# Score matmuls of a top-k attention: the second parts of q stored twice, so that the contraction is 128 rows

## The chip, the cores and the metric

One core of one Trainium2 chip runs the kernel. The metric is the device time of one execution in microseconds (us). Three executions of the kernel before took 955.11, 954.19 and 959.35 us; the median is 955.11 us.

## What is computed

Attention over q, k, v of 2 batches, 8 heads, 576 positions and 64 numbers per head, in which every row of scores keeps only its 32 largest; its output (1152 tokens of 512 numbers) goes through a mixture layer with one expert of eight per token, and then through a mixture of four experts that all tokens use.

```python
scores = scale * np.matmul(q, k.transpose(0, 1, 3, 2))
kth = np.partition(scores, -top_k, axis=-1)[..., -top_k:-top_k + 1]
scores = np.where(scores >= kth, scores, -1e9)
...
attn = attn / (np.sum(attn, axis=-1, keepdims=True) + 1e-09)
x = np.matmul(attn, v)
...
h = np.maximum(x[mask] @ w1[e], 0.0)
out[mask] = gate_w[mask, None] * (h @ w2[e])
...
out += p[:, e:e + 1] * (np.maximum(x @ w1[e], 0.0) @ w2[e])
```

## The kernel before, in words

The 1152 tokens are nine tiles of 128. Tile 4 (`MIX`) holds the end of batch 0 and the start of batch 1. The tiles form three groups: (0, 1), (2, 3, 4) and (5, 6, 7, 8). The attention of group 0 runs alone at the start. After that the mixture layers of group g run on TensorE while the attention of group g+1 is laid between them, so that TensorE's instruction stream alternates between first layers (`hps`, L1120), second layers (`y`, L1093) and pieces of attention. The last group's layers run alone at the end.

**Precision by parts.** An fp32 operand is written as two parts (a rounded one and the rest), and a product is a sum of products of parts. In the mixture layers these are `whi`, `wlo` of the weights (ScalarE rounds at L996, GpSimd or VectorE subtracts at L1004) and `hhi`, `hlo` of the hidden values (ScalarE L1134, VectorE L1137). A second layer needs `hlo` two f-tiles (blocks of 128 hidden values) after it was made from.

**Attention.** The unit of work is a tile and a pair of heads, 36 units in all. For each unit:

- `q_tr` (L313 to L319) transposes the pair's parts of q on TensorE into the bank `qtp`, and `q_ev` (L321 to L335) copies them on ScalarE into `qs`.
- `sc_mm` (twice, once per head) calls `scores_mm` (L265 to L277): for each half of the 576 keys two matmuls of 288 columns (in tile 4 four, for its two batches) accumulate in the bank `sps`. The first contracts 128 rows: the first part of q, which stands twice, against k's two parts (64 rows each, stacked). The second contracts 64 rows: the second part of q against the first part of k alone. `sc_ev` (L460) copies the sums on ScalarE to `s_sb`.
- VectorE finds the 32 largest of each row by four rounds of MAX8 and MATCH_REPLACE8 (L472, L481), ScalarE takes the exponential, VectorE masks it (`e`, L494), ScalarE and GpSimd make two half-precision parts (`pbuf`), a DMA transposes them (`pt`, L523), and TensorE multiplies by v (`pv`, L548).

The banks of `qtp` and `sps` come from one pool with a single buffer (`ps_s`), so a transpose waits until the scores before it are copied out, and the other way round. The pool of `qs` has 4 buffers, that of the rows of q (`qrow`) one.

Per tile, `q_hi` (ScalarE, L302) rounds q into the first copy, `q_lo` (L307) has GpSimd subtract and ScalarE write the first part's second copy (L311). For tile 0 this is done by pieces in `q_part` (L617).

**Order.** `at_step(n, fn)` puts each piece in a plan by half steps, and the plan is written out in that order; an attention step is emitted whenever the cost estimate of the mixture layers (`pace`) says one is due. Unit j starts at b0 = 8j. Its `q_tr` is at b0-16, `q_ev` at b0-15, `sc_mm` at b0-5 and b0-3, each `sc_ev` one step later; a tile's `q_hi` is at b0-21 and `q_lo` at b0-20 of its first unit. Each engine runs its instructions strictly in the order written.

```python
for n, r in ((i, slice(0, 128)), (2, slice(64 * i, 64 * i + 64))):
    nc.tensor.matmul(out=ps[:, f, 0:HALF], lhsT=qq[r, n, :],
                     rhs=kst[r, h, b * S + f * HALF:b * S + (f + 1) * HALF],
                     start=(j == 0), stop=(j == n_mm - 1))
```

Of the kernel before, what the change touches and what calls it, by code (L numbers as in the profile page):

```python
# [49 lines left out]
def kernel(  # L50
# [41 lines left out]
    def h_bank(shape, name):  # L92
        """A bank for a first layer's sums."""
        return ps_h.tile(shape, F32, tag="h", name=name)

    def side_bank(shape, name):
        """A bank for a side job's sums: of its own where there is one."""
        if not h_extra:
            return h_bank(shape, name)
        h_count[0] += 1  # L100
        return h_extra[h_count[0] % len(h_extra)].tile(shape, F32, tag="h", name=name)

    with tc.manual_schedule():
# [44 lines left out]
        def emit_const_math():  # L148
# [10 lines left out]
            # how many tokens each slot has room for: all, or its windows' rows; nothing beyond the slots  # L159
# [60 lines left out]
        def attention(at, start):  # L220
# [6 lines left out]
            qst_p = pool("qst", 4)  # L227
# [37 lines left out]
            def scores_mm(t, h, i, qs):  # L265
                ps = ps_s.tile([128, 2, 512], F32, tag="s", name="sps")
                bs = batches(t)
                for f in range(2):
                    n_mm = 2 * len(bs)
                    j = 0  # L270
                    for qq, b in zip(qs, bs):
                        for n, r in ((i, slice(0, 128)), (2, slice(64 * i, 64 * i + 64))):
                            nc.tensor.matmul(out=ps[:, f, 0:HALF], lhsT=qq[r, n, :],  # L273
                                             rhs=kst[r, h, b * S + f * HALF:b * S + (f + 1) * HALF],
                                             start=(j == 0), stop=(j == n_mm - 1))
                            j += 1
# [13 lines left out]
            # rows of q, k, v: load, split, transpose  # L290
# [6 lines left out]
            # q by pairs of heads: the first part of each twice, then the second parts; against k's two parts, which  # L297
            # an odd head has the other way round
            def q_first(t, n):
                return row["q", t][:, :, 0:4, :].rearrange("p c (i a) d -> p c i a d", a=2)[:, :, :, n, :]  # L300

            def q_hi(t):  # L302
                row["q", t] = row_p.tile([128, H // 2, 6, D], F32R, tag="qrow", name="qrow")
                nc.scalar.activation(out=q_first(t, 0), in_=raw["q", t].rearrange("p (c i) d -> p c i d", i=2),
                                     func=ACTF.Copy)

            def q_lo(t, eng):  # L307
                eng.tensor_tensor(out=row["q", t][:, :, 4:6, :],
                                  in0=raw.pop(("q", t)).rearrange("p (c i) d -> p c i d", i=2),
                                  in1=q_first(t, 0).bitcast(F32), op=ALU.subtract)  # L310
                nc.scalar.activation(out=q_first(t, 1), in_=q_first(t, 0).bitcast(F32), func=ACTF.Copy)  # L311
# [9 lines left out]
            def q_ev(j):  # L321
                t, hp = units[j]
                ps = st[j].pop("qps")
                if t != MIX:
                    qs = qst_p.tile([128, 3, 128], F32R, tag="qs", name="qs")
# [4 lines left out]
                for b in range(2):  # L330
                    qs = qst_p.tile([128, 3, 128], F32R, tag="qs", name=f"qs{b}")
# [87 lines left out]
            def v_scale(b, n):  # L419
                """The scale and its inverse, from the bound's exponent; the instructions apart."""  # L420
# [32 lines left out]
            # per pair of heads  # L453
# [102 lines left out]
            def row_factor(t, n):  # L556
                """The rows' factor, its three instructions apart."""
# [25 lines left out]
            # the first pair, by pieces: head 0's block of k, the two heads' last columns, head 1's block  # L583
            def first_ld():
# [19 lines left out]
                row["q", t] = row_p.tile([128, H // 2, 6, D], F32R, tag="qrow", name="qrow")  # L604
# [12 lines left out]
            def q_part(cs, part, eng=None):  # L617
                t = units[0][0]
                q0 = raw["q", t].rearrange("p (c i) d -> p c i d", i=2)[:, cs]
                if part == 1:  # L620
                    eng.tensor_tensor(out=row["q", t][:, cs, 4:6, :], in0=q0, in1=q_first(t, 0)[:, cs].bitcast(F32),
                                      op=ALU.subtract)
                else:
                    nc.scalar.activation(out=q_first(t, part // 2)[:, cs], in_=q0, func=ACTF.Copy)

            # the first pair's chain, and what it needs
            for n, fn, *args in (
                    (-40, first_ld), (-37, k_ld, 1, 0), (-34, emit_const_loads),
                    (-30, k_part, 0, 0), (-29, k_part, 0, 1), (-30, q_part, slice(0, 1), 0),
                    (-29, q_part, slice(0, 1), 1, nc.vector), (-29, q_part, slice(0, 1), 2),  # L630
                    (-28, k_part, 2, 0), (-27, k_part, 2, 1),
# [4 lines left out]
                    (-22, q_part, slice(1, H // 2), 1, nc.gpsimd),  # L636
# [5 lines left out]
            for j in range(NP):  # L642
# [73 lines left out]
        # what goes between VectorE's instructions that wait for one another, and whether side jobs go twice as often  # L716
# [3 lines left out]
        def gate(g, xhi, xlo, i0, i1):  # L720
            """Expert choice and gate of tiles i0..i1 of the group, and their counts."""
# [747 lines left out]
```

## Time and profile before

| | kernel before |
|---|---|
| time, median of 3 (lowest to highest) | 955.11 us (954.19 to 959.35) |
| profiled execution: span, first to last instruction | 952.8 us |
| TensorE matmul busy | 873.3 us, 92% |
| TensorE weight load busy | 707.2 us, 74% |
| VectorE busy | 662.1 us, 69% |
| ScalarE busy | 489.0 us, 51% |
| GpSimd busy | 535.7 us, 56% |
| DMA | 129.60 MB, mean 136 GB/s |
| mean granted TensorE clock | 0.955 of full |

The median is 2.3 us over the span of the profiled execution, whose own time beyond its span isn't given. In the profile PE is TensorE's matmuls, PEld its weight loads, DVE VectorE, ACT ScalarE, POOL GpSimd, SP the queue that issues most DMAs. L273 is line 273 of the kernel. Matmul ends are modelled: the distance between starts tells more than one matmul's length. A busy share is an average over the whole run; the stages below have different limits.

### The profile page before, as it was taken

To read this page: it belongs to the slowest core of one execution; us is meant where nothing else is said; L and a number is where in the kernel's file an instruction comes from. 1 tells how busy PE (TensorE), PEld (TensorE's weight loads), DVE (VectorE), ACT (ScalarE), POOL (GpSimd) and SP (SyncE) were. 2 spreads that over 40 slices of the span, in tenths; PEclk is the share of its full clock that TensorE was granted. 3 is DMA by queue.
4 is the path that set the end of the run, shared out by engine and by line. 5 is a ranking of instruction groups with operands and counts; after the bars stand their busy time and mean duration, and the time that the engine had idled before them with its cause. 6 is when DMAs were issued, how large, how long until landed. Compare 5 with 4: busy or idle time off the path is not lost.

```text
span 952.8 us, 15053 instructions
## 1 busy us (share of the span) xinstructions
PE 873.3 (92%) x5241; PEld 707.2 (74%) x5241; DVE 662.1 (69%) x1309; ACT 489.0 (51%) x1007; POOL 535.7 (56%) x469
## 2 busy tenths in 40 slices
PE   5776677999999998899999999997999999999996
PEld 3554465887877886788877888786889778888884
DVE  5998979998968999799979888974334341112222
ACT  5766654665766654567735665442356332422320
POOL 3553456886766976567857665573535533343330
PEclk9995578999999999799999999999999999999999
DMA  7354544766655663847756555453546622323201
GB/s 129 70 107 91 133 115 120 207 184 166 161 146 130 167 184 108 203 139 218 208 128 170 139 132 136 138 146 100 165 144 222 188 89 96 104 89 111 89 23 49
DMA packets 197627, 129.60 MB, mean 136 GB/s; under 512 B 129122, under 2 KB 172130, under 8 KB 197540
## 3 DMA queue, kind: packets, MB, share of 16 engines
q1 hardware_dynamic: 196500, 125.12, 48.7%
q0 software_dynamic: 1040, 3.41, 1.4%
q8 instruction: 43, 0.70, 0.3%
q14 instruction: 44, 0.36, 0.1%
HBM read 98.62 MB, written 6.30 MB: 110 GB/s over the span
## 4 chain that ended last, share of the span: by engine, by line
PE 77%; DVE 11%; DMA 3%; issue 2%; ACT 2%; SPq 2%; POOL 2%; POOLq 0%; ACTq 0%; DVEq 0%
PE hps L1120 31%; PE y L1093 30%; PE sps L273 8%; PE pv L548 4%; DVE m L472 3%; DVE w L481 3%; PE xtp L1022 1%; PE qtp L318 1%; DMA wraw<-in_moe_w_dram 1%; DMA xg<-x_scr,ixi 1%; PE ktp L370 1%; DVE e L494 1%; DMA pt<-pbuf 1%; POOL wlo L1004 1%; SPq L399 0%
## 5 line engine op out<-in xcount | busy, mean ns | idle before, releaser
L1004 POOL TENSOR_TENSOR wlo<-wraw,whi 128x512 fp32r<-128x512 f32 x278 | 368.9, 1346 | 282.2 <-ACT whi L996 236.1
L1137 DVE SCALAR_TENSOR_TENSOR hlo<-hps,hhi 128x256 fp32r<-128x256 f32 (+3 forms) x168 | 84.0, 500 | 210.0 <-ACT hhi L1134 209.7
L1134 ACT ACTIVATE hhi<-hps 128x256 fp32r<-128x256 f32 (+3 forms) x168 | 75.4, 449 | 268.5 <-PE hps L1120 260.5
L996 ACT ACTIVATE whi<-wraw 128x512 fp32r<-128x512 f32 x336 | 193.3, 624 | 23.0 <-DMA wraw<-in_moe_w_dram 22.8
L1093 PE MATMUL y<-whi,hhi 128*128 128x512 f32 x440 | 180.7, 411 | 0.0
L1120 PE MATMUL hps<-x,whi 128*128 128x256 f32 (+2 forms) x768 | 168.4, 342 | 6.4 <-DVE hlo L1137 5.1
L1093 PE MATMUL y<-wlo,hhi 128*128 128x512 f32 x440 | 173.5, 394 | 0.0
L1093 PE MATMUL y<-whi,hlo 128*128 128x512 f32 x440 | 173.1, 394 | 0.0
L472 DVE MAX8 m<-w 128x8 f32<-128x576 f32 x216 | 154.1, 743 | 0.0
L1120 PEld LDWEIGHTS hps<-x,whi 128*128 128x128 f32 x768 | 130.2, 191 | 21.2 <-DVE hlo L1137 5.5
L273 PE MATMUL sps<-kst,qs 128*128 128x288 f32 x320 | 120.7, 432 | 15.7 <-ACT qs L326 7.9
L518 POOL TENSOR_TENSOR pbuf<-e,pbuf 128x576 f16<-128x576 f32 (+1 forms) x80 | 107.2, 1340 | 47.6 <-ACT pbuf L509 45.0
L273 PEld LDWEIGHTS sps<-kst,qs 128*128 128x128 f32 x320 | 67.2, 210 | 66.6 <-issue 22.0
L481 DVE MATCH_REPLACE8 w<-m,w 128x576 f32<-128x576 f32 x144 | 105.9, 739 | 0.0
L1093 PEld LDWEIGHTS y<-whi,hlo 128*128 128x128 f32 x440 | 83.1, 189 | 18.5
L1093 PEld LDWEIGHTS y<-whi,hhi 128*128 128x128 f32 x440 | 83.8, 190 | 17.0
L1093 PEld LDWEIGHTS y<-wlo,hhi 128*128 128x128 f32 x440 | 83.7, 190 | 11.9
L1120 PE MATMUL hps<-x,wlo 128*128 128x256 f32 (+2 forms) x384 | 85.3, 341 | 0.0
L494 DVE SCALAR_TENSOR_TENSOR e<-s_sb,m,e 128x576 f32<-128x576 f32 x72 | 80.1, 1139 | 2.0 <-ACT e L489 2.0
L1120 PEld LDWEIGHTS hps<-x,wlo 128*128 128x128 f32 x384 | 65.8, 192 | 5.4
L548 PEld LDWEIGHTS <-pt 128*128 128x128 f16 (+3 forms) x1200 | 49.2, 106 | 27.1 <-issue 14.1
L548 PE MATMUL pv<-vst,pt 128*128 128x64 f16 (+3 forms) x1200 | 62.1, 204 | 6.1 <-DMA pt<-pbuf 4.8
(179 smaller groups left out, 1044.1 us busy)
## 6 DMA issues: line engine op xcount, KB each, us to landing
wraw<-in_moe_w_dram SPq DMA_DIRECT2D x168, 512.0 KB, 3.8
x_scr<-xrow SPq DMA_DIRECT2D x9, 256.0 KB, 2.0
out_dram<-acc SPq DMA_DIRECT2D x9, 256.0 KB, 2.2
kraw<-in_k_dram SPq DMA_DIRECT2D x16, 128.0 KB, 3.2
vraw<-in_v_dram SPq DMA_DIRECT2D x8, 256.0 KB, 3.4
qraw<-in_q_dram SPq DMA_DIRECT2D x7, 256.0 KB, 5.6
y_scr<-yr SPq DMA_DIRECT2D x6, 256.0 KB, 2.8
pt<-pbuf SPq DMA_TRANSPOSE x72, 4.1
```

What stands on the lines that cost most here:

```text
L273: nc.tensor.matmul(out=ps[:, f, 0:HALF], lhsT=qq[r, n, :], rhs=kst[r, h, b * S + f * HALF:b * S + (f + 1) * HALF], start=(j == 0), stop=(j ...
L472: nc.vector.max(out=z["m"][:, i, 8 * r:8 * r + 8], in_=z["s", i] if r == 0 else z["w"][i])
L481: nc.vector.match_replace(out=z["w"][i], in_to_replace=z["m"][:, i, 8 * r:8 * r + 8], in_values=z["s", i] if r == 0 else z["w"][i], imm_va ...
L494: nc.vector.scalar_tensor_tensor(out=z["e"][i], in0=z["s", i], scalar=z["m"][:, i, TOPK - 1:TOPK], in1=z["e"][i], op0=ALU.is_ge, op1=ALU.mult)
L518: nc.gpsimd.tensor_tensor(out=pb[r, 1, o:o + S], in0=z["e"][i][r], in1=pb[r, 0, o:o + S], op=ALU.subtract)
L548: nc.tensor.matmul(out=po[r, h, :], lhsT=l, rhs=rr, start=(n == 0), stop=(n == len(mms) - 1))
L996: nc.scalar.activation(out=hi, in_=src, func=ACTF.Copy)
L1004: eng.tensor_tensor(out=lo, in0=src, in1=hi.bitcast(F32), op=ALU.subtract)
L1093: nc.tensor.matmul(out=ys[i][0:rows, :], lhsT=l[:, cs], rhs=r[:, 0, :], start=(f == f0 and m == 0), stop=(f == f1 - 1 and m == 2))
L1120: nc.tensor.matmul(out=hp[:, 0:n], lhsT=l[:, c, :], rhs=r[:, c, x0:x0 + n], start=(m == 0), stop=(m == 3 * KD - 1))
L1134: nc.scalar.activation(out=hhi, in_=hp[:, 0:n], func=ACTF.Relu)
L1137: nc.vector.scalar_tensor_tensor(out=hlo, in0=hp[:, 0:n], scalar=0.0, in1=hhi.bitcast(F32), op0=ALU.max, op1=ALU.subtract)
```

## The change

The rows of q hold the second part twice as well (8 blocks of 64 per pair of heads where 6 stood). So there are four transposes per unit where three stood, `qs` is a third wider, and the second matmul of each pair is the same shape as the first: 128 rows, the second part of q against both parts of k. It so adds the product of the two second parts, which the kernel before left out. A new ScalarE copy, `q_two`, writes the second copy. `qs` has 3 buffers where it had 4. For tile 4 and the first unit of tile 5 `q_tr` moves from b0-16 to b0-9, and tile 5's `q_hi` and `q_lo` from b0-21 and b0-20 to b0-16 and b0-15. Comments and docstrings are emptied as well.

```diff
-            qst_p = pool("qst", 4)
+            qst_p = pool("qst", 3)
...
-                        for n, r in ((i, slice(0, 128)), (2, slice(64 * i, 64 * i + 64))):
-                            nc.tensor.matmul(out=ps[:, f, 0:HALF], lhsT=qq[r, n, :],
-                                             rhs=kst[r, h, b * S + f * HALF:b * S + (f + 1) * HALF],
+                        for n in (i, 2 + i):
+                            nc.tensor.matmul(out=ps[:, f, 0:HALF], lhsT=qq[:, n, :],
+                                             rhs=kst[:, h, b * S + f * HALF:b * S + (f + 1) * HALF],
...
-            def q_first(t, n):
-                return row["q", t][:, :, 0:4, :].rearrange("p c (i a) d -> p c i a d", a=2)[:, :, :, n, :]
+            def q_at(t, part, n):
+                return row["q", t].rearrange("p c (m i a) d -> p c m i a d", i=2, a=2)[:, :, part, :, n, :]
...
-                row["q", t] = row_p.tile([128, H // 2, 6, D], F32R, tag="qrow", name="qrow")
+                row["q", t] = row_p.tile([128, H // 2, 8, D], F32R, tag="qrow", name="qrow")
...
+            def q_two(t):
+                nc.scalar.activation(out=q_at(t, 1, 1), in_=q_at(t, 1, 0).bitcast(F32), func=ACTF.Copy)
...
-                ps = ps_s.tile([128, 3, 128], F32, tag="s", name="qtp")
+                ps = ps_s.tile([128, 4, 128], F32, tag="s", name="qtp")
...
-                for n in range(3):
+                for n in range(4):
...
-                    qs = qst_p.tile([128, 3, 128], F32R, tag="qs", name="qs")
+                    qs = qst_p.tile([128, 4, 128], F32R, tag="qs", name="qs")
...
+                elif part == 3:
+                    nc.scalar.activation(out=q_at(t, 1, 1)[:, cs], in_=q_at(t, 1, 0)[:, cs].bitcast(F32),
+                                         func=ACTF.Copy)
...
+                    (-28, q_part, slice(0, 1), 3),
...
-                    (-22, q_part, slice(1, H // 2), 1, nc.gpsimd),
+                    (-22, q_part, slice(1, H // 2), 1, nc.gpsimd), (-20, q_part, slice(1, H // 2), 3),
...
-                    at_step(b0 - 16 if j > 1 else -4, q_tr, j)
-                    at_step(b0 - 15 if j > 1 else -3, q_ev, j)
+                    late = t == MIX or (t == MIX + 1 and hp == 0)
+                    b2 = -4 if j == 1 else b0 - 9 if late else b0 - 16
+                    at_step(b2, q_tr, j)
+                    at_step(b2 + 1, q_ev, j)
...
-                    at_step(b0 - 21, q_hi, t)
-                    at_step(b0 - 20, q_lo, t, nc.gpsimd)
+                    b3 = b0 - 16 if t == MIX + 1 else b0 - 21
+                    at_step(b3, q_hi, t)
+                    at_step(b3 + 1, q_lo, t, nc.gpsimd)
+                    at_step(b3 + 3, q_two, t)
```

## Rows read from the trace of the kernel before

**Rows 1.** The page, part 4: the chain that ended last, shares by engine.

```profile
PE 77%; DVE 11%; DMA 3%; issue 2%; ACT 2%; SPq 2%; POOL 2%; POOLq 0%; ACTq 0%; DVEq 0%
```

**Rows 2.** Stages: length, busy PE, PEld, DVE, ACT, POOL (instructions), clock, DMA share, GB/s.

```profile
170.00:240.00 70.00, 68.59 (x494) 56.56 (x492) 62.88 (x119) 44.54 (x96) 52.97 (x43) 1.00 0.66 177
240.00:356.00 116.00, 115.22 (x884) 92.17 (x883) 101.56 (x203) 73.31 (x163) 89.83 (x72) 1.00 0.62 162
400.00:500.00 100.00, 97.75 (x655) 80.07 (x655) 91.30 (x164) 60.80 (x127) 67.36 (x55) 0.97 0.65 176
500.00:612.00 112.00, 110.96 (x692) 90.58 (x692) 99.47 (x190) 63.43 (x129) 72.26 (x62) 1.00 0.54 138
```

**Rows 3.** The chain in order of time, 312 to 340 us: start, length, instructions.

```profile
312.71 2.41 PE sps L273 x8
...
326.87 1.11 PE sps L273 x4
327.97 0.89 PE y L1093 x3
328.87 1.43 PE hps L1120 x12
330.30 0.69 PE y L1093 x3
...
339.15 0.48 PE qtp L318 x3
```

**Rows 4.** Timeline of TensorE's weight loads, 326 to 329 us: start, length, instructions.

```profile
326.93 0.83 PEld L273 LDWEIGHTS sps<-kst,qs 64*128 64x128 f32 x3 [0.26 <-issue]
...
328.48 0.65 PEld L1120 LDWEIGHTS hps<-x,whi 128*128 128x128 f32 x4
```

**Rows 5.** The score matmuls (L273) alone in the stages: length, PE, PEld, clock, DMA share, GB/s.

```profile
170.00:240.00 70.00, 11.54 (x36) 6.58 (x36) 1.00 0.66 177
240.00:356.00 116.00, 25.90 (x80) 14.79 (x80) 1.00 0.62 162
400.00:500.00 100.00, 14.54 (x44) 8.27 (x43) 0.97 0.65 176
500.00:612.00 112.00, 16.51 (x52) 9.62 (x52) 1.00 0.54 138
```

**Rows 6.** VectorE's waits, 170 to 240 us: waiter, releaser, us in total, times, longest.

```profile
DVE wlo L1004 <- ACT whi L996: 1.8, 1, 1.8
DVE x L1027 <- ACT x L1024: 1.7, 2, 1.4
```

**Rows 7.** VectorE's waits, 240 to 356 us.

```profile
DVE hlo L1137 <- ACT hhi L1134: 8.0, 8, 2.0
DVE wlo L1004 <- ACT whi L996: 2.7, 1, 2.7
DVE lg L740 <- PE lp L737: 1.9, 1, 1.9
```

**Rows 8.** VectorE's waits, 400 to 500 us.

```profile
DVE wlo L1004 <- ACT whi L996: 2.7, 2, 2.3
DVE xs L929 <- ACT xs L928: 2.3, 1, 2.3
DVE x L1027 <- ACT x L1024: 1.6, 2, 0.8
```

**Rows 9.** The chain at 23 and 154 us.

```profile
23.32 2.21 PE sps L273 x4
...
154.52 2.93 PE hps L1120 x12
```

**Rows 10.** VectorE's waits, 0 to 25 us.

```profile
DVE m L472 <- ACT s_sb L460: 4.6, 2, 2.3
```

**Rows 11.** Timelines of ScalarE and of GpSimd: tile 3's parts of q.

```profile
143.34 0.64 ACT L311 ACTIVATE qrow<-qrow 128x512 fp32r<-128x512 f32 x1
...
147.02 1.27 POOL L308 TENSOR_TENSOR qrow<-qraw,qrow 128x512 fp32r<-128x512 f32 x1
```

More of the change, by code (lines that the diff above doesn't have):

```diff
@@ L295, in ld @@
                 raw[kind, t] = load_rows(src, t, io_p, kind + "raw")
-            def q_first(t, n):
-                return row["q", t][:, :, 0:4, :].rearrange("p c (i a) d -> p c i a d", a=2)[:, :, :, n, :]
+            def q_at(t, part, n):
+                return row["q", t].rearrange("p c (m i a) d -> p c m i a d", i=2, a=2)[:, :, part, :, n, :]
             def q_hi(t):
-                row["q", t] = row_p.tile([128, H // 2, 6, D], F32R, tag="qrow", name="qrow")
-                nc.scalar.activation(out=q_first(t, 0), in_=raw["q", t].rearrange("p (c i) d -> p c i d", i=2),
+                row["q", t] = row_p.tile([128, H // 2, 8, D], F32R, tag="qrow", name="qrow")
+                nc.scalar.activation(out=q_at(t, 0, 0), in_=raw["q", t].rearrange("p (c i) d -> p c i d", i=2),
                                      func=ACTF.Copy)
             def q_lo(t, eng):
-                eng.tensor_tensor(out=row["q", t][:, :, 4:6, :],
+                eng.tensor_tensor(out=q_at(t, 1, 0),
                                   in0=raw.pop(("q", t)).rearrange("p (c i) d -> p c i d", i=2),
-                                  in1=q_first(t, 0).bitcast(F32), op=ALU.subtract)
-                nc.scalar.activation(out=q_first(t, 1), in_=q_first(t, 0).bitcast(F32), func=ACTF.Copy)
+                                  in1=q_at(t, 0, 0).bitcast(F32), op=ALU.subtract)
+                nc.scalar.activation(out=q_at(t, 0, 1), in_=q_at(t, 0, 0).bitcast(F32), func=ACTF.Copy)
+            def q_two(t):
+                nc.scalar.activation(out=q_at(t, 1, 1), in_=q_at(t, 1, 0).bitcast(F32), func=ACTF.Copy)
             def q_tr(j):
                 t, hp = units[j]
-                ps = ps_s.tile([128, 3, 128], F32, tag="s", name="qtp")
+                ps = ps_s.tile([128, 4, 128], F32, tag="s", name="qtp")
                 qf = row["q", t][:, hp].rearrange("p a d -> p (a d)").bitcast(F32)
-                for n in range(3):
+                for n in range(4):
                     nc.tensor.transpose(out=ps[:, n, :], in_=qf[:, n * 128:(n + 1) * 128], identity=ident)
@@ L330, in q_ev @@
                 for b in range(2):
-                    qs = qst_p.tile([128, 3, 128], F32R, tag="qs", name=f"qs{b}")
+                    qs = qst_p.tile([128, 4, 128], F32R, tag="qs", name=f"qs{b}")
                     z0, c0 = (64, 0) if b == 0 else (0, 64)
@@ L603, in first_ld @@
                 row["k", 0, 0] = k_p.tile([128, 5, 4, D], F32R, tag="krow", name="krow")
-                row["q", t] = row_p.tile([128, H // 2, 6, D], F32R, tag="qrow", name="qrow")
+                row["q", t] = row_p.tile([128, H // 2, 8, D], F32R, tag="qrow", name="qrow")
             def k_part(n, part):
@@ L620, in q_part @@
                 if part == 1:
-                    eng.tensor_tensor(out=row["q", t][:, cs, 4:6, :], in0=q0, in1=q_first(t, 0)[:, cs].bitcast(F32),
+                    eng.tensor_tensor(out=q_at(t, 1, 0)[:, cs], in0=q0, in1=q_at(t, 0, 0)[:, cs].bitcast(F32),
                                       op=ALU.subtract)
+                elif part == 3:
+                    nc.scalar.activation(out=q_at(t, 1, 1)[:, cs], in_=q_at(t, 1, 0)[:, cs].bitcast(F32),
+                                         func=ACTF.Copy)
                 else:
-                    nc.scalar.activation(out=q_first(t, part // 2)[:, cs], in_=q0, func=ACTF.Copy)
+                    nc.scalar.activation(out=q_at(t, 0, part // 2)[:, cs], in_=q0, func=ACTF.Copy)
             for n, fn, *args in (
```

## The prediction

> **What bounds the kernel now.** I read the chain that ended last, then the busy times by stage, then the waits in each stage. The chain lies on TensorE for 77% of the span and on VectorE for 11% [rows 1]. By stages TensorE is close to full from 170 to 240, 240 to 356, 400 to 500 and 500 to 612 us: it is idle for 1.4, 0.8, 2.3 and 1.0 us there. VectorE is behind it by little: it is idle for 7.1, 14.4, 8.7 and 12.5 us in the same stages [rows 2]. So two engines are nearly balanced while attention and mixture layers run together: whatever TensorE saves there counts only until VectorE has no idle time left. Before 154 us the top-k on VectorE sets the pace, between 356 and 400 us the routing does, and after 612 us no attention is left that the change could touch.
>
> **What a score matmul costs.** In the chain, twelve first-layer matmuls of 256 columns take 1.43 us, 0.119 us each, and three second-layer ones of 512 columns take 0.69 us, 0.23 us each [rows 3]. On the line through both, 288 columns of 128 rows take 0.119 + 32/256 x 0.111 = 0.133 us. The four matmuls of a score call take 1.11 us, and the three `y` behind them 0.89 where 0.69 is usual. A call so costs 1.31 us, more than twice what its columns need. The excess goes with the alternation of 128 and 64 rows: the weight load for a 64-row matmul sits idle for 0.26 us before it starts, while four loads of the first layer, all 128 rows, go in 0.65 us [rows 4].
>
> The Trainium skill, TensorEngine Tiling (Array Packing), Key Properties, says that a change of tiling mode, not of the tile alone, drains TensorE; it agrees with these rows.
>
> After the change every matmul on that path has 128 rows, so I take the 128-row price: 4 x 0.133 = 0.53 us a call, a saving of 0.78 us. Bounds: nothing if the wait belongs to the weights and not to the rows (a rival below), and the whole 0.78. I take the whole, since the first-layer rows are the nearest in shape and in parts. A call of tile 4 has eight matmuls: 2.41 us plus the same 0.20 behind it, less 8 x 0.133, saves 1.55 us [rows 3].
>
> **Parts of the sum, stage by stage.** The score matmuls number 36, 80, 44 and 52 in the four stages [rows 5]; tile 4's 64 fall into the second. That is 9 plain calls, 4 plain and 8 of tile 4, 11 and 13 plain. TensorE saves 7.0, 3.1 + 12.4 = 15.5, 8.6 and 10.1 us. Each unit (two calls) pays a fourth transpose. Three take 0.48 us in the chain [rows 3], so 0.16 us; over 4.5, 6, 5.5 and 6.5 units 0.7, 1.0, 0.9 and 1.0 us. Net on TensorE: 6.3, 14.5, 7.7 and 9.1 us, together 37.6 us.
>
> Now what VectorE lets through. Of its idle time I keep the waits whose releaser is not sped up. These are 1.8 us for rounded weights and 1.7 us for rounded rows in the first stage [rows 6], so 3.6 us of 7.1 can go. In the second they are 2.7 and 1.9 us [rows 7], so 9.8 us of 14.4 can go; 8.0 us of that waits for ScalarE's `hhi`, which waits for TensorE, so it is the kind of wait that a faster TensorE shortens. In the third they are 2.7, 2.3 and 1.6 us [rows 8], so 2.1 us of 8.7. In the fourth I keep none, and TensorE's 9.1 us is the smaller number. Taking the smaller of the two engines in each stage: 3.6 + 9.8 + 2.1 + 9.1 = 24.6 us.
>
> **The start.** There the clock is at its low level of 1.2 GHz by the durations: a score call takes 2.21 us, and twelve first-layer matmuls 2.93 us, 0.244 each [rows 9], so 288 columns about 0.275 and a call 1.1 us, a saving of 1.1 us. VectorE's first two MAX8 wait 4.6 us for the first two calls [rows 10]. Two savings come to 2.2 us, less one cold transpose and a wider copy in the first chain (by the rows for the warm ones some 0.4 us): 1.8 us. Later in this stage VectorE is what is waited for, and I count nothing: 23 calls get cheaper there behind the top-k.
>
> **ScalarE and GpSimd.** `q_two` is a copy of 128x512 for each tile, 0.64 us like the one that already stands there [rows 11]. A wider `q_ev` adds less than that per unit. ScalarE is idle for 43 of 116 us and 49 of 112 us in the fullest stages [rows 2], so I cost both at nothing; without that cover it would be at most 8 x 0.64 us, and some tenths per unit. But `q_two` also adds a wait: ScalarE can't go on until GpSimd has subtracted. Behind it in ScalarE's queue are `whi`, `hhi` and `s_sb`, and TensorE waits for those. For tile 3 GpSimd ends at 148.3 us, and ScalarE's copy before it starts at 143.3 us [rows 11]. `q_two` comes two steps after that copy; a unit of eight steps takes 70/4.5 = 15.6 us by rows 5, so it comes 3.9 us later, at 147.2 us. The wait is some 1.1 us for this tile, and VectorE is the bound there; I count nothing.
>
> **The moved steps.** For tile 4 and the first unit of tile 5 the transpose is four steps before the scores, some 8 us, instead of eleven; the copies in between are four of a few tenths, so they stay hidden. At tile 5 two transposes follow each other through the one bank, and TensorE must wait for ScalarE's copy between them. I price that once, 1 us, from the 0.64 us copy plus its place in the queue. The three buffers of `qs` hold as many bytes as the four before and, with tile 4's later steps, are free in time. `q_ev` waiting for a buffer is bounded by one score call, 1.3 us, at one place. Transfers, bytes and DMA issues are unchanged.
>
> **Sum.** 24.6 + 1.8 - 1.0 = 25.4 us off a profiled span of 952.8 us. The runs stand 2.3 us above the span; carried over, the median of 955.1 becomes 929.7, and I say 929 us.
>
> **Rivals.**
>
> *All of TensorE's saving arrives.* VectorE may run late without harm, because `hlo` is used two f-tiles later. Then 37.6 + 1.8 and about 2 us between 356 and 400 come off: 914 us. For it: VectorE's lateness has room inside a stage. Against: at the end of each stage the rows of the next layer need VectorE. Chance 0.10.
>
> *Less fits.* The same copies, subtractions and top-k come closer together, GpSimd is busy for 90 of 116 us already [rows 2], and weights come later. If only half of 25.4 us gets through: 942 us. Chance 0.13.
>
> *The load, not the rows.* The weight load of a matmul may have to wait until the matmul before it has left the same rows. Then 128-row matmuls pay a load (0.65/4 = 0.16 us at the least, [rows 4]) plus 0.133, about 0.30 us as now, nothing is saved, and 36 transposes of 0.16 us are added, of which the 22.5 in the four stages matter: 955 to 959 us. Against it, the first layers are 128 rows each and go at 0.119 us with their loads, less than one load and one matmul in series. The Trainium skill, TensorE: Matmul & The Clock Gate, Part 3: Packing small matmuls — row/col tiling, says that weight loads overlap with running matmuls only where the row groups differ; that speaks against the change and would give this time. The trace disagrees, with the 0.119 us of the first layers. Chance 0.03.
>
> *Slower.* `q_two` holds ScalarE. GpSimd's subtraction for tile 3 begins 3.7 us after ScalarE's neighbouring copy [rows 11]; if in a fuller schedule it begins some 5 us later still at each of seven tiles, ScalarE stands for 5 us each time, `hhi` and `whi` come late, and 35 us are lost against 25 won: 965 us. It decides where GpSimd ends more than about 4 us after that copy starts, and by more than two f-tiles' worth of slack. Against: the tile in the rows is over that by one us only. Chance 0.05.
>
> **How the numbers follow.** The forecast, 920 to 938 us around 929, has 0.69. The range of 913 to 945 us takes in the two neighbours on the fast side and leaves out the last two rivals and a tail on each side, together under 0.2. About 0.5% is what a measurement of this kernel can tell from no change. Faster by more: 0.69 + 0.10 + 0.13, less a little for a half that shrinks further: 0.90. Same: 0.04. Slower: 0.06.
>
> **What would show it right or wrong.** Right: score matmuls of one shape, 128 rows, x320; a call in the warm stages at about 0.53 us; no idle of 0.26 us before their loads; `y` behind them at 0.69 us for three; 144 transposes. VectorE's idle in the stage of tile 4 shrinks to about 5 us, its waits for `hhi` nearly go, and TensorE begins to wait for `hlo`. ScalarE's `q_two` waits for GpSimd by about a microsecond at most. The stages before 154 us and after 612 us keep their lengths but for the first microseconds. Wrong: calls that stay near 1.1 us (the load), long waits of ScalarE at `q_two`, a granted clock below 1.00 in the four stages, or a total at 914 us with VectorE still idle.

## The result, and the profile after

The changed kernel takes 924.9 us (median of 4 runs, 922.85 to 927.44) where the kernel before, on the same chip, takes 954.85 (4 runs, 954.19 to 959.35): a ratio of 0.9681, 95% interval 0.9653 to 0.971. The forecast was 929, with a range of 913 to 945.

The page of the changed kernel, parts 1 and 5: the span, the busy times, and the score matmuls as one group (busy us, mean ns, then idle before and its releaser).

```profile
span 921.1 us, 15133 instructions
...
PE 815.3 (89%) x5277; PEld 696.2 (76%) x5277; DVE 659.2 (72%) x1309; ACT 496.6 (54%) x1017; POOL 534.6 (58%) x469
...
L273 PE MATMUL sps<-kst,qs 128*128 128x288 f32 x320 | 64.8, 333 | 19.5 <-ACT s_sb L465 9.5
```

All 320 score matmuls now have one shape. TensorE's busy time fell from 873.3 to 815.3 us, 58.0 us, of which 31.7 reached the span (952.8 to 921.1). VectorE and GpSimd are busy as long as before, ScalarE 7.6 us longer. The spans are those of one execution each; by the medians the gain is 30 us. The question is where the other 26 us went.

TensorE's timeline after the change: a plain call at 515 us, and one of tile 4 at 258 us.

```profile
258.34 1.23 PE L273 MATMUL sps<-kst,qs 128*128 128x288 f32 x8
259.41 0.39 PE L1107 MATMUL y<-whi,hhi 128*128 128x512 f32 x1
...
515.10 0.69 PE L273 MATMUL sps<-kst,qs 128*128 128x288 f32 x4
515.62 0.85 PE L1134 MATMUL hps<-x,whi 128*128 128x384 f32 x4
```

The four weight loads of the plain call:

```profile
514.87 0.68 PEld L273 LDWEIGHTS sps<-kst,qs 128*128 128x128 f32 x4
```

Read the starts. The plain call takes 515.62 - 515.10 = 0.52 us, where 1.11 and 0.20 behind it stood [rows 3]; the call of tile 4 takes 259.41 - 258.34 = 1.07 us, where 2.41 and 0.20 stood. That is 0.13 us for each matmul of 128 rows and 288 columns. Their four loads go in 0.68 us without an idle stretch between them.

To see where the time came off, cut both traces where the same work happens: the transposes of a tile's rows of x (`xtp<-xrow`) and those of a group's sums (`xtp<-acc`). Stages of the kernel before: the start to tile 1's rows, tile 1's rows to group 0's sums, tile 2's rows to tile 4's, tile 4's rows to group 1's sums (in two pieces), tile 5's rows to tile 7's. Columns as in [rows 2].

```profile
0.00:126.88 126.88, 87.26 (x445) 58.39 (x445) 111.75 (x250) 79.31 (x163) 55.59 (x81) 0.79 0.52 107
126.88:234.10 107.22, 98.18 (x658) 81.46 (x659) 94.79 (x189) 64.29 (x139) 84.81 (x68) 0.94 0.62 167
239.98:355.45 115.47, 114.69 (x880) 91.65 (x878) 101.03 (x202) 73.33 (x163) 89.85 (x72) 1.00 0.62 162
355.45:400.00 44.55, 36.88 (x241) 30.78 (x239) 39.51 (x94) 22.29 (x50) 28.00 (x24) 0.91 0.56 142
400.00:492.64 92.64, 92.64 (x612) 76.20 (x611) 85.57 (x156) 57.72 (x121) 66.08 (x54) 0.97 0.70 190
500.68:590.69 90.01, 88.97 (x547) 72.63 (x545) 79.22 (x149) 51.53 (x104) 59.08 (x51) 1.00 0.56 144
```

The same stages of the changed kernel.

```profile
0.00:120.98 120.98, 67.42 (x457) 53.97 (x457) 110.37 (x250) 81.82 (x167) 56.83 (x81) 0.63 0.55 112
120.98:223.96 102.98, 91.05 (x661) 79.63 (x662) 94.27 (x189) 64.70 (x137) 83.20 (x68) 0.92 0.64 164
230.19:339.81 109.62, 102.69 (x886) 89.52 (x884) 101.32 (x201) 75.79 (x167) 89.39 (x72) 0.98 0.67 171
339.81:383.00 43.19, 36.63 (x253) 31.62 (x252) 40.16 (x97) 23.91 (x52) 28.89 (x25) 0.92 0.52 144
383.00:471.07 88.07, 82.24 (x609) 71.69 (x607) 84.59 (x154) 57.48 (x120) 64.30 (x54) 1.00 0.80 200
481.21:561.89 80.68, 80.68 (x551) 71.64 (x550) 76.72 (x145) 51.94 (x104) 57.71 (x49) 1.00 0.56 150
```

| from and to (before) | length before, after | came off |
|---|---|---|
| start to tile 1's rows, 0 to 126.88 | 126.88, 120.98 | 5.9 |
| to group 0's sums, 234.10 | 107.22, 102.98 | 4.2 |
| to tile 2's rows, 239.98 | 5.88, 6.23 | -0.4 |
| to tile 4's rows, 355.45 | 115.47, 109.62 | 5.9 |
| to group 1's sums, 492.64 | 137.19, 131.26 | 5.9 |
| to tile 5's rows, 500.68 | 8.04, 10.14 | -2.1 |
| to tile 7's rows, 590.69 | 90.01, 80.68 | 9.3 |
| to the end | 362.1, 359.2 | 2.9 |

TensorE's busy time tells where the rest went. In the stages from tile 1's rows to tile 7's it fell by 7.1, 12.0, 10.7 (both pieces) and 8.3 us, 38.1 in all, where 37.6 was forecast for four stages cut a little otherwise; 25.3 of that came off. At the start it fell by 19.8 us, and 5.9 came off.

In the last of the full stages TensorE is still busy throughout (80.68 of 80.68 us), and all of its saving arrives. In the stage of tile 4 it is now idle for 6.9 us where it was idle for 0.8, and of 12.0 us that it saved 5.9 arrive. The waits of TensorE in that stage after the change (waiter, releaser, us in total, times, longest) tell on what.

```profile
PE pv L553 <- DMA pt<-pbuf: 4.2, 3, 2.7
PE xtp L1036 <- DVE xrow L577: 0.9, 1, 0.9
PE y L1107 <- ACT acc L1186: 0.6, 1, 0.6
```

Before, there was one wait of 0.8 us on that list, for `xrow`. Now TensorE waits at tiles' ends for the DMA that transposes the probabilities. And VectorE's waits there, to be held against [rows 7]:

```profile
DVE wlo L1018 <- ACT whi L1010: 2.4, 1, 2.4
DVE xrow L577 <- PE pv L553: 2.2, 1, 2.2
DVE hlo L1151 <- ACT hhi L1148: 1.9, 3, 0.9
```

The wait for `hhi` went from 8.0 to 1.9 us, as was foreseen; the one of `xrow` for `pv` grew from 0.6 to 2.2, the other end of the late transposing DMA.

### The profile page after: what moved, and what is told of

Same layout as the page of the kernel before. It is cut to its first block, busy times and chain, and to the rows that moved or that the text cites. A ratio compares the mean times of both kernels' runs of the same rounds, so it can differ in the third digit from the quotient of the medians.

```text
span 921.1 us, 15133 instructions
## 1 busy us (share of the span) xinstructions
PE 815.3 (89%) x5277; PEld 696.2 (76%) x5277; DVE 659.2 (72%) x1309; ACT 496.6 (54%) x1017; POOL 534.6 (58%) x469
## 5 line engine op out<-in xcount | busy, mean ns | idle before, releaser
L1018 POOL TENSOR_TENSOR wlo<-wraw,whi 128x512 fp32r<-128x512 f32 x278 | 364.4, 1332 | 251.1 <-ACT whi L1010 212.6
L1107 PE MATMUL y<-whi,hhi 128*128 128x512 f32 x440 | 177.6, 404 | 1.0 <-ACT acc L1186 0.6
L523 POOL TENSOR_TENSOR pbuf<-e,pbuf 128x576 f16<-128x576 f32 (+1 forms) x80 | 109.5, 1368 | 48.9 <-ACT pbuf L514 45.3
L273 PE MATMUL sps<-kst,qs 128*128 128x288 f32 x320 | 64.8, 333 | 19.5 <-ACT s_sb L465 9.5
L514 ACT ACTIVATE pbuf<-e 128x576 f16<-128x576 f32 (+1 forms) x80 | 54.2, 678 | 38.4 <-DVE e L499 38.0
L273 PEld LDWEIGHTS sps<-kst,qs 128*128 128x128 f32 x320 | 52.9, 212 | 27.7 <-ACT s_sb L465 12.9
```

The costliest lines, as they stand in the source:

```text
L273: nc.tensor.matmul(out=ps[:, f, 0:HALF], lhsT=qq[:, n, :], rhs=kst[:, h, b * S + f * HALF:b * S + (f + 1) * HALF], start=(j == 0), stop=(j ...
L523: nc.gpsimd.tensor_tensor(out=pb[r, 1, o:o + S], in0=z["e"][i][r], in1=pb[r, 0, o:o + S], op=ALU.subtract)
L1018: eng.tensor_tensor(out=lo, in0=src, in1=hi.bitcast(F32), op=ALU.subtract)
L1107: nc.tensor.matmul(out=ys[i][0:rows, :], lhsT=l[:, cs], rhs=r[:, 0, :], start=(f == f0 and m == 0), stop=(f == f1 - 1 and m == 2))
```

## The experiments

The theory: TensorE pays for each change between 64 and 128 rows, the change removes these, and VectorE, which was behind TensorE by little, takes part of what is won. Rivals: the load and not the rows; all of the saving arrives; the copies that double the second part eat some of it.

**1. Group the rows, keep them (`e1_order`).** The kernel before, with the same matmuls in another order: first those of 128 rows, then those of 64.

```diff
-                for f in range(2):
-                    n_mm = 2 * len(bs)
...
-                        for n, r in ((i, slice(0, 128)), (2, slice(64 * i, 64 * i + 64))):
+                for n, r in ((i, slice(0, 128)), (2, slice(64 * i, 64 * i + 64))):
+                    for qi, (qq, b) in enumerate(zip(qs, bs)):
+                        for f in range(2):
```

> The kernel before with the score matmuls in another order: first all those of 128 rows of a call, then all those of 64, so that the row count changes twice a call instead of four times (twice instead of eight times in tile 4). Shapes, counts and results are the same. If the change of rows is what costs: (1.31 - 0.53) / 4 = 0.195 us for each change, a plain call falls from 1.31 to about 0.92 us and one of tile 4 from 2.61 to 1.45, TensorE saves 37 x 0.39 + 8 x 1.16 = 24 us in the four stages, and with VectorE close behind 14 to 22 us of it arrive: 932 to 941 us. If a matmul of 64 rows is slow in itself, or its load is, whatever stands before it: no change, 952 to 958 us.

Measured: 933.15 us (930.39 to 936.5) beside 954.98, ratio 0.9784, 0.9749 to 0.9819. TensorE's timeline of this kernel, a plain call and what follows it:

```profile
328.88 0.88 PE L271 MATMUL sps<-kst,qs 128*128 128x288 f32 x4
329.69 0.50 PE L1090 MATMUL y<-whi,hhi 128*128 128x512 f32 x1
330.03 0.40 PE L1090 MATMUL y<-wlo,hhi 128*128 128x512 f32 x1
```

The call takes 329.69 - 328.88 = 0.81 us and the `y` behind it 0.34 where 0.23 is usual: 0.92 us in all. Nothing is left out, the same rows and the same bytes are loaded, and the number of changes of rows went from four to two. With none it is 0.53. So (1.31 - 0.53)/4 = 0.195 us for each change, and 0.53 + 2 x 0.195 = 0.92. A call of tile 4, with two changes where eight stood, confirms it:

```profile
242.08 1.42 PE L271 MATMUL sps<-kst,qs 128*128 128x288 f32 x8
243.43 0.50 PE L1090 MATMUL y<-whi,hhi 128*128 128x512 f32 x1
```

It takes 1.35 us and 0.11 behind it, 1.46 in all, where 2.61 stood and 1.45 was expected. The price belongs to the change of rows between neighbours; that a matmul has 64 rows costs nothing in itself. The new order also uses the same weights twice in a row and takes turns between the two halves of `sps`, but the changed kernel does neither, and its calls are the cheapest.

**2. The row count alone (`e2_cross`).** The kernel before with one edit. The second matmul of a head takes all 128 rows that stand there, so that it adds the product of the second part of the pair's other head with k's second part, a term of the size of the one that the kernel before leaves out. No copies, no fourth transpose, no moved step.

```diff
-                        for n, r in ((i, slice(0, 128)), (2, slice(64 * i, 64 * i + 64))):
+                        for n, r in ((i, slice(0, 128)), (2, slice(0, 128))):
```

> The kernel before with one edit: the second matmul contracts all 128 rows of the block that holds the second parts of both heads, with no doubling of q, no fourth transpose, no added copy, no moved step. It adds the product of the other head's second part with k's second part, a term of the size of those that the kernel leaves out. If the row count alone carries the gain: as fast as the changed kernel or faster by what the doubling costs, up to 22 transposes of 0.16 us in the four stages and the ScalarE waits for GpSimd: 919 to 926 us. If the doubling, the moved steps or the later copies carry part of the gain: 930 us or more.

Measured: 918.69 us (914.89 to 926.43), ratio 0.965, 0.96 to 0.97. The page's group of score matmuls:

```profile
L273 PE MATMUL sps<-kst,qs 128*128 128x288 f32 x320 | 65.9, 338 | 18.0 <-ACT s_sb L460 8.8
```

The row count alone carries the whole gain. Whether the rest of the change costs something was asked again, with both kernels on one chip:

**3. The changed kernel (`a2_after`) beside the row count alone (`e6_cross`).**

> The changed kernel again, beside the two kernels of this call. Expected by every theory: 925 us, ratio 0.968.

> The kernel before with the one edit of the second matmul's rows (128 instead of 64, against what stands there: the other head's second part, a product of the size of what the kernel leaves out), beside the change on one chip. Theory: the row count alone carries the gain; the doubled rows cost 36 transposes of 0.16 us (5.8 us of TensorE), nine copies of 0.64 us on ScalarE and the moved steps, so this kernel is 4 to 8 us below the change, about 919 us. Rival: the doubling is hidden behind VectorE, and the two are within 2 us.

Measured: 924.43 us (919.97 to 924.89), ratio 0.9684, 0.9662 to 0.9706, and 919.16 us (916.82 to 922.93), ratio 0.9634, 0.9613 to 0.9655. The doubling with its transposes, copies and moved steps costs 5.3 us by the medians; the two intervals of the ratio lie apart by a hair, so the size is known no better than to a few us. It happens to be about 36 transposes of 0.16 us, but it isn't spread like them. From tile 2's rows to tile 4's, first `e6_cross`, then `a2_after`:

```profile
229.51:334.20 104.69, 100.38 (x880) 87.96 (x878) 101.35 (x202) 73.61 (x164) 90.36 (x72) 1.00 0.68 177
228.51:336.57 108.06, 101.21 (x885) 88.26 (x884) 100.70 (x201) 75.79 (x167) 89.38 (x72) 1.00 0.67 171
```

In this stage, which has tile 4's own steps and the first of tile 5's, the changed kernel is 3.4 us longer (4.9 and 5.0 in two more profiles of it, 109.62 and 109.72 us). From tile 5's rows to tile 7's it is 0.5 us longer (80.69 against 80.15). Which of the three parts costs it wasn't tried apart.

**4. Less work for VectorE (`e3_before_top24`, `e4_after_top24`).** In both kernels the fourth round of the top-k is left out, so that rows keep 24 scores and not 32.

```diff
-                    out=z["e"][i], in0=z["s", i], scalar=z["m"][:, i, TOPK - 1:TOPK], in1=z["e"][i],
+                    out=z["e"][i], in0=z["s", i], scalar=z["m"][:, i, TOPK - 9:TOPK - 8], in1=z["e"][i],
...
-                    for r in range(4):
+                    for r in range(3):
...
-                        if r < 3:
+                        if r < 2:
```

> The kernel before without the fourth round of the top-k search: only the 24 largest scores are kept (left out: 72 MAX8 and 72 MATCH_REPLACE8, 107 us of VectorE). If TensorE bounds the four stages, mostly the start and the routing stage shorten, some 25 to 45 us: 910 to 930 us. If VectorE bounds the whole attention, the time falls by 70 us or more: under 885 us.

> The changed kernel without the fourth round, as the run before. VectorE now has room in all stages. If VectorE took the rest of TensorE's saving, the difference to the kernel before without the fourth round grows from 30 us to the full saving, 37 to 48 us. If the 30 us were all that TensorE saves, or if something else (weights, GpSimd) took the rest, the difference stays at 25 to 33 us.

Measured: 2209.55 us (2208.03 to 2212.05) and 2171.21 us (2167.82 to 2171.91). The totals expected were missed by far, and for a reason outside the question: with other attention rows the routing fills an expert beyond its places, and a pass over all experts, which the kernel holds ready for that, runs at the end of both. The difference stands, 38.3 us where the full top-k leaves 30, and so do the stages ahead of that pass. Three stages of the kernel before with the shorter top-k, tile 1's rows to group 0's sums, tile 2's rows to tile 4's and tile 5's rows to tile 7's:

```profile
121.47:227.79 106.32, 97.82 (x658) 81.35 (x659) 78.35 (x159) 64.47 (x139) 82.47 (x68) 0.93 0.64 169
235.13:350.61 115.48, 114.70 (x881) 91.64 (x879) 81.83 (x162) 73.33 (x162) 87.65 (x71) 1.00 0.60 162
...
491.55:580.24 88.69, 88.69 (x547) 72.59 (x545) 60.98 (x117) 50.95 (x103) 57.82 (x49) 1.00 0.55 144
```

The same three of the changed kernel with the shorter top-k:

```profile
111.33:210.55 99.22, 89.18 (x660) 78.97 (x661) 79.55 (x159) 64.82 (x137) 83.06 (x68) 0.93 0.66 179
216.78:323.49 106.71, 100.78 (x885) 88.44 (x884) 85.57 (x162) 75.89 (x167) 89.59 (x72) 1.00 0.69 174
...
461.40:542.07 80.67, 80.67 (x552) 71.61 (x551) 61.18 (x115) 51.80 (x104) 58.49 (x49) 1.00 0.61 156
```

Where VectorE is the bound and is relieved, more of TensorE's saving arrives: 10.1 us up to tile 1's rows (121.47 and 111.33) where it was 5.9, and 7.1 from there to group 0's sums where it was 4.2. In the stage of tile 4 the kernel before takes 115.48 us with 34 us of VectorE's idle time and 115.47 with 14.4: there TensorE alone sets the length. After the change it is 106.71 us against 109.62, at most 2.9 us that VectorE gives back (1.4 beside the 108.06 of `a2_after`, whose clock there was 1.00 and not 0.98). But 6 us of TensorE's idle time stay, and 3.7 of them are again `pv` waiting for the DMA that transposes `pbuf`. So VectorE is not the only taker.

**5. More work for VectorE (`e8_before_max`, `e9_after_max`).** In both kernels the first MAX8 of each head is written twice from tile 2 on.

```diff
                 nc.vector.max(out=z["m"][:, i, 8 * r:8 * r + 8], in_=z["s", i] if r == 0 else z["w"][i])
+                if r == 0 and t > 1:
+                    nc.vector.max(out=z["m"][:, i, 8 * r:8 * r + 8], in_=z["s", i] if r == 0 else z["w"][i])
```

> The kernel before with the first MAX8 of every head written twice for tiles 2 to 8: 56 more VectorE instructions of 0.74 us, 41 us in all, about 33 us of them in the four stages, where VectorE was idle for 7.1, 14.4, 8.7 and 12.5 us (43 us together, some 25 of them usable). Theory (two engines nearly balanced; VectorE's idle is what TensorE's saving can use): the idle time takes much of it, so the time rises by 12 to 22 us, to 967 to 977. Rival (VectorE is not what limits, TensorE is): up to 5 us, 955 to 960.

> The same 56 MAX8 in the changed kernel, where VectorE's idle in the stages is down to about 19 us. Theory: most of the 41 us arrives, 30 to 40, so 955 to 965 us, and the gain of the change falls from 30 to 10 to 18 us, of which 6 come from the start that is untouched. Rival (VectorE does not limit after the change either): about 930 us, the gain stays at 30.

Measured: 970.96 us (967.27 to 980.45), ratio to the kernel before 1.0192, 1.0123 to 1.026, and 953.65 us (949.21 to 954.67), ratio 0.9972, 0.995 to 0.9993. The same 42.6 us of VectorE's work cost 16.4 us before the change and 28 to 29 after it (953.65 against 924.43 to 925.51 us, the lowest and the highest of three measurements). The second number misses what was expected, 30 to 40, by 1 to 2 us; the gain that is left, 17.3 us, is within it. The stages of both, first the kernel before with the added MAX8:

```profile
128.70:239.69 110.99, 99.27 (x659) 81.89 (x660) 103.37 (x201) 64.09 (x139) 82.71 (x68) 0.92 0.59 154
245.57:361.50 115.93, 115.07 (x880) 91.46 (x878) 107.81 (x214) 73.45 (x163) 90.41 (x72) 1.00 0.60 161
```

and the changed kernel with it:

```profile
123.81:234.78 110.97, 93.94 (x661) 81.08 (x661) 103.20 (x201) 64.78 (x137) 82.54 (x68) 0.90 0.58 152
241.01:353.99 112.98, 104.27 (x885) 90.34 (x884) 109.21 (x213) 75.85 (x167) 89.26 (x72) 0.97 0.65 166
```

These two stages each got about a dozen more instructions on VectorE, some 9 us. From tile 1's rows to group 0's sums they cost 3.8 us before (110.99 against 107.22) and 8.0 after (against 102.98), and both kernels now take the same 111 us: VectorE sets it. In the stage of tile 4 they cost 0.5 and 3.4 us. From tile 4's rows to group 1's sums it is 4.8 and 10.8 us (141.98 against 137.19, 142.03 against 131.26), again to the same length; but two more profiles of the changed kernel take 130.05 and 135.98 us there, so the second number can be 6 to 12. From tile 5's rows to tile 7's it is 0.1 and 1.3. So before the change VectorE took about half of such an addition in its stride or more. After it VectorE is at its limit from tile 1's rows to group 0's sums, and from tile 4's rows to group 1's probably too.

**6. The start (`e12_two_calls`).** The kernel before, 128 rows in the first two score calls alone (in these the term of `e2_cross` is added).

```diff
-                        for n, r in ((i, slice(0, 128)), (2, slice(64 * i, 64 * i + 64))):
+                        for n, r in ((i, slice(0, 128)), (2, slice(0, 128) if t == 0 and h < 2 else slice(64 * i, 64 * i + 64))):
```

> The kernel before with 128 rows in the second matmul of the first two score calls alone (tile 0, heads 0 and 1); all others stay at 64. The prediction priced the start by these two calls alone, at 1.8 us, while the start of the changed kernel came 6.4 us earlier. Theory: the other 4.5 us come from the later cold calls on the way to tile 0's rows, so here tile 0's rows come 1.5 to 2.5 us earlier than before (76.28 us), and the time falls by about 2, to 952. Rival: the first two calls bring all of it (VectorE runs on without a break from its first MAX8): 6 us earlier, 948 us.

Measured: 951.82 us (949.3 to 957.04) beside 955.39, ratio 0.9967, 0.9945 to 0.9989; tile 0's rows come at 73.67 us instead of 76.28, 2.6 us earlier. The wait of MAX8 for the first scores fell from 4.6 us [rows 10] to 2.6. The first theory holds, a little above its upper end: of the 6.4 us that the changed kernel gains up to this point, less than half comes from the two calls that were priced.

The two rows are from one profile each; three profiles of the changed kernel gain 6.4, 6.2 and 5.1 us up to here. Part of what is still missing shows in VectorE's waits up to 77 us: at tile 0's end its `xrow` waits for `pv`, and in the changed kernel that wait isn't there.

```profile
DVE xrow L572 <- PE pv L548: 1.9, 1, 1.9
```

TensorE's timeline of this kernel: the second of the two changed calls, with 128 rows throughout, then the next two, of 64 and 128 rows, and a later one of these at 45 us with what follows it.

```profile
9.23 1.33 PE L273 MATMUL sps<-kst,qs 128*128 128x288 f32 x4 [0.69 <-ACT kst L386]
...
18.32 1.37 PE L273 MATMUL sps<-kst,qs 128*128 128x288 f32 x4 [1.76 <-ACT qs L326]
20.43 2.22 PE L273 MATMUL sps<-kst,qs 128*128 128x288 f32 x4 [0.74 <-ACT s_sb L460]
...
44.81 2.22 PE L273 MATMUL sps<-kst,qs 128*128 128x288 f32 x4 [0.74 <-ACT s_sb L460]
46.96 2.11 PE L548 MATMUL pv<-vst,pt 128*128 128x64 f16 x30
```

**7. The same remedy for the values (`e7_pv_rows`, `e10_after_pv`).** Three of the 15 `pv` matmuls of a head contract 64 rows. Zeros in `vst` and `pbuf` fill them up to 128, first on top of `e6_cross`, then on top of the changed kernel.

```diff
+                if t in (MIX, MIX + 1) and 2 * hp + i < NPB:
+                    nc.gpsimd.memset(pb[(slice(64, 128) if t == MIX else slice(0, 64)), :, 0:64], 0.0)
...
-                            kr = slice(0, 128) if c < 4 else slice(0, 64)
+                            kr = slice(0, 128)
...
-                            kr = slice(64, 128) if c == 0 else slice(0, 128)
+                            kr = slice(0, 128)
...
+            at_step(-20, lambda: nc.gpsimd.memset(vst[64:128, MIX], 0.0))
```

> The same, and the pv matmuls too are made 128 rows throughout (three of the 15 of a call contract 64 rows; zeroed columns of pbuf and zeroed rows of vst fill them up). A pv call in the warm stages takes 0.64 us plus 0.11 behind it. If the price of a change of rows is general (0.195 us for each of the two changes in a call), a call comes to about 0.40 us, 0.35 saved. 72 calls then free some 20 us of TensorE. Theory: VectorE is nearly full in the stages (idle 0.6, 3.3, 4.6 and 3.7 us), so little of it arrives: 912 to 917 us. Rival (TensorE's saving arrives): about 900 us. Rival (float16 matmuls of 64 columns do not pay for a change of rows): calls stay at 0.75 us and the time at 919.

Measured: 913.48 us (911.43 to 918.82), ratio 0.9591, 0.9565 to 0.9617; 5.7 us below `e6_cross` by the medians, with intervals that overlap by a hair. TensorE's timeline of `e2_cross`, where the `pv` calls are as in the kernel before, and then of this kernel:

```profile
259.76 0.72 PE L548 MATMUL pv<-vst,pt 128*128 128x64 f16 x15
260.40 0.51 PE L1093 MATMUL y<-whi,hhi 128*128 128x512 f32 x1
260.74 0.40 PE L1093 MATMUL y<-wlo,hhi 128*128 128x512 f32 x1
```

```profile
259.67 0.61 PE L550 MATMUL pv<-vst,pt 128*128 128x64 f16 x15
260.11 0.48 PE L1096 MATMUL y<-whi,hhi 128*128 128x512 f32 x1
260.43 0.39 PE L1096 MATMUL y<-wlo,hhi 128*128 128x512 f32 x1
```

A call goes from 0.64 to 0.44 us and the extra time of the `y` behind it from 0.11 to 0.09 (0.34 and 0.32 against 0.23): 0.22 us saved, where 0.35 was expected. Two changes of rows so cost 0.11 us each here, not 0.195, and 0.09 behind the call belongs to something else than rows.

> The changed kernel with the pv matmuls made 128 rows too (the zeroed columns of pbuf and rows of vst, as in e7_pv_rows). There a pv call came from 0.75 to 0.53 us and the time fell by some 5.7 us beside e6_cross. Theory: the same here, 924.4 less 4 to 7 us, 917 to 921 us. Rival (VectorE and the transposing DMA of pbuf let nothing more through after the change): 923 to 926 us.

> The changed kernel once more, as the partner of e10_after_pv on the same chip: 924 to 925 us.

Measured: 916.26 us (913.66 to 919.35), ratio 0.9602, 0.9578 to 0.9627, and for the changed kernel 925.51 us (922.3 to 928.79), ratio 0.9697, 0.9671 to 0.9723. The intervals lie apart, and 9.3 us are more than the 4 to 7 expected. Of some 72 x 0.22 = 16 us that TensorE saves by this estimate, more than half arrives, though VectorE had little room left. This kernel computes what the changed kernel does and beats both of the kernels compared here.

## Why the prediction was right, and where its terms were off

**The price of a score call: right.** 1.31 us to 0.53 was forecast; 0.52 was measured, and in tile 4 1.07 us where 8 x 0.133 = 1.06 was said. `e1_order` shows what the price is attached to, the change of rows. The rival that the weight load is what costs fell: the loads are as many as before and larger. The Trainium skill, TensorEngine Tiling (Array Packing), Key Properties, says that a change of tiling mode drains TensorE; the runs agree and give the price here, 0.195 us for each change. The Trainium skill's rule in TensorE: Matmul & The Clock Gate, Part 3: Packing small matmuls — row/col tiling, that loads overlap only with matmuls of other row groups, would have left the time as it was. The runs speak against it: matmuls of 128 rows start 0.13 us apart, and four of their loads take 0.68 us, 0.17 us each, so that a load has no room between two starts and runs beside a matmul of the same rows.

**Balance with VectorE: right in kind.** 58 us of busy time went and 32 arrived. Two pairs of runs show the mechanism: the same added MAX8 cost 16 us before the change and 28 to 29 after, and with a shorter top-k 38.3 us arrive and not 30. Both neighbours of the forecast have fallen: 914 us with all of the saving arriving, and 942 us with half of the forecast gain.

**By stage: the sum was right, its terms less so.**

| term | forecast | measured | two more profiles of the changed kernel |
|---|---|---|---|
| start | 1.8 | 5.9 | 5.8, 4.4 |
| first full stage | 3.6 | 4.2 | 6.1, 4.7 |
| tile 4's stage, less moved steps | 9.8 - 1.0 | 5.9 | 7.4, 5.8 |
| 356 to 493 us, and on to tile 5's rows | 2.1 | 5.9 - 2.1 | -2.1, 4.4 |
| from tile 5's rows, to 591 us and beyond | 9.1 | 9.3 + 2.9 | 9.3 + 3.6, 9.3 + 1.1 |

The last column is `a2_after` and `a3_after`, each against the one profile of the kernel before. That the sum came within 5 us of the 30 measured is in part luck: the start and the last stages gave more than was said, and tile 4's stage gave less.

- *The start* was mis-sized because only VectorE's first two waits were priced, and the later cold calls were put behind VectorE. `e12_two_calls` gives the two calls 2.6 us up to tile 0's rows, against the 1.8 forecast. The rest of the 6.4 has to come from what follows: the wait of `xrow` for `pv`, 1.9 us in that run, is gone in the changed kernel, and the ten calls up to that point are cheaper by about 1 us each where the clock is low. Which of them VectorE waited for was not tried one by one.
- *Tile 4's stage* was over-estimated by 1 to 3 us. That the wait for `hhi` is "the kind of wait that a faster TensorE shortens" was right (8.0 to 1.9 us). With the row count alone, `e6_cross`, 10.8 us come off this stage (115.47 to 104.69; 10.9 in `e2_cross`), more than the 9.8 that VectorE was said to let through. So the term that was mis-sized is the moved steps with the doubled rows: 1.0 us was costed, and the changed kernel is 3.4 to 5.0 us behind `e6_cross` here, with 6.9 us of TensorE's idle time where that has 4.3. The changed kernel waits there for ScalarE's copies (`acc`, `s_sb` and `qs`, 1.4 us in all), which `e6_cross` doesn't. What ends most of TensorE's waits in both is the transposing DMA. In `e6_cross`:

```profile
PE pv L548 <- DMA pt<-pbuf: 4.0, 4, 2.8
```

  At a tile's end the chain from the mask over `pbuf` and this DMA to `pv` and `xrow` has a length of its own, which shows once TensorE gets there earlier: no wait before the change, 4.0 us with the row count alone, 4.2 in the changed kernel, and 3.7 with the shorter top-k, so it is more than VectorE's lateness.
- *356 to 493 us, and on to tile 5's rows* can't be sized by one profile. The kernel before takes 145.2 us from tile 4's rows to tile 5's, the changed kernel 141.4, 147.3 and 140.8 in three profiles, so between 2.1 us more and 4.4 less. The forecast's 2.1 less lies among them. Part of what differs is when transfers land. In the longest (`a2_after`) TensorE waits for the gather of x's rows, as in the kernel before (2.9 us), in the other two not at all:

```profile
PE xgp L940 <- DMA xg<-x_scr,ixi: 4.1, 1, 4.1
```

  The 2.1 us lost between group 1's sums and tile 5's rows may be of this kind too. There VectorE adds the gathered results of the experts, and TensorE waits for it 5.1 us in the first profile of the changed kernel, 5.7 and 3.2 in the others, and 1.6 in the kernel before. But `e12_two_calls`, which from here on is the kernel before, waits 2.8 us and takes 10.3 us for this piece, like the changed kernel's 10.1 and not like the 8.0 of the kernel before. So that loss isn't shown to come from the change.
- *The last stage* was a little low: the 9.1 us stood for all of it up to 612 us, and 9.3 were there at 591. The step holds, though: TensorE is full, and its saving is the gain. The attention behind that (tile 8's rows, 645.62 against 615.05 us) brings 1.8 of the other 2.9.

**What was costed at nothing**, `q_two`, was nearly that. It waits for GpSimd 2.9 us in all over the run, 1.9 at the longest (a later tile than the one argued about), so the slower rival, some 35 us lost there, never came near. The doubling as a whole costs 5 us, by `e6_cross`. The sum had less than half of that: 1.0 for moved steps, some 0.4 at the start, and of the 3.6 us of transposes only the last stage's 1.0, since in the other stages VectorE's smaller number was taken.

**Signs that did not come.** VectorE's idle time in the stage of tile 4 was to shrink to about 5 us; it is 8.3 (3.3 in `e6_cross`). TensorE was to wait for `hlo` there; it does for 0.3 us. The start was to keep its length but for the first microseconds; it is 5.9 us shorter. A clock below 1.00 in the stages was to speak against the prediction: in tile 4's stage it was 0.98 in the first profile and 1.00 in `a2_after`, and in the stage after it 0.97 where it had been 0.95.

## What to carry to other kernels

Where matmuls of 64 and of 128 rows follow each other, count the changes, not the rows: put equal row counts together, or fill up with rows that cost no load of their own. An operand that stands there anyway, or zeros, will do: here matmuls of 128 rows took 0.119, 0.13 and 0.23 us for 256, 288 and 512 columns. When an engine on the path gets cheaper, ask stage by stage what is late next, and look there for transfers with a length of their own (here the transposing DMA at a tile's end), not only at the second busiest engine. And take a stage's length from more than one profile before a term of a few us is called right or wrong: the same kernel's stage with the gathers varied by 6.5 us.

## What the runs showed of the hardware

- At the full clock a change of row count costs 0.195 us between matmuls of four-byte operands and 288 columns, and 0.11 us between `pv`'s half-precision ones of 64 columns. Why they differ is open.
- At the low clock a change of rows costs more, but not twice as much. At 45 us `e12_two_calls` shows a granted clock of 0.50, and a call of mixed rows takes 2.15 us from its start to that of the next matmul; in the changed kernel, at 0.50 as well, it takes 1.13 (44.04 to 45.17), four times 0.28. Over the three changes inside a call that is 0.34 us each, against 0.195 at the full clock.
- The clock changed within the start and took the price of a call with it: in the lines of `e12_two_calls` above, the call of mixed rows at 18.32 takes 1.37 us at a granted clock of 1.00 (its loads 0.19 us each), and the next of the same kind, 2 us later, 2.22 us at 0.50 (0.29).
- The profile of the kernel before records a granted clock of 1.00 at 45 us too, with calls of 2.22 us, which the other profiles show at 0.50. In `e12_two_calls` the call of 128 rows at 9.23 us takes 1.33 us beside a recorded 1.00, as long as one in the changed kernel at 0.50 (18.91 us). So the recorded clock of the start is to be held against the length of a known matmul. The mean clock of the kernel before, 0.955 beside 0.929 after, is therefore no sign that the change slowed the clock.
